# Two gMLP scalars: from GpSimd broadcasts to single elements that TensorE spreads over the partitions

## The chip, the cores and the metric

The kernel runs on one core of a Trainium2 chip. The metric is device time in microseconds (us). The chip's executions of this kernel fall into two close groups: in 35 runs of the kernel before, 7 lie at 667.7 to 668.0 us and 28 at 668.8 to 669.2. All count as fast.

The traces show where the groups part. The last 16 matmuls of the program took 1.25 us at a granted TensorE clock of 1.00 and 2.29 to 2.30 us at 0.50. From the last landing to the end that makes 3.60 to 3.76 us or 4.60 to 4.80 us.

## The reference

One decode step: layer norm, cached attention (batch 4, 32 heads, 4096 keys of 128) and a gMLP, summed.

```python
xn = _layernorm(x, axis=-1)
return x + _A_ref(xn, A_k_cache, A_v_cache, A_wq, A_wo) + _B_ref(xn, B_w_in, B_w_sp, B_b_sp, B_w_out)

def _B_ref(x, w_in, w_sp, b_sp, w_out):      # cut
    z = _gelu(jnp.einsum('bsd,df->bsf', x, w_in))
    z1 = z[..., :Fh]; z2 = _layernorm(z[..., Fh:], axis=-1)
    g = jnp.einsum('ts,bsf->btf', w_sp, z2) + b_sp[None, :, None]
    return jnp.einsum('bsf,fd->bsd', z1 * g, w_out)
```

The sequence has length 1, so `w_sp` and `b_sp` are one number each. They are the two scalars.

## The kernel before

The loads of weights, keys and values all go through SyncE's queue into one large buffer `kv`, in a fixed order. The scalars come through GpSimd, copied from one element in memory to all 128 partitions; much later a cast and one DVE instruction use them.

```python
nc.sync.dma_start(out=wq, in_=A_wq.rearrange("(p c) n -> p c n", c=DC))      # 5 MB, first load
nc.scalar.dma_start(out=x_bf, in_=x_flat)
...
sb_bf = const.tile([P, 2], BF16)
nc.gpsimd.dma_start(out=sb_bf[:, 0:1], in_=B_w_sp.rearrange("a b -> (a b)").to_broadcast((P, 1)))
nc.gpsimd.dma_start(out=sb_bf[:, 1:2], in_=B_b_sp.to_broadcast((P, 1)))
...                                                                         # w_in, w_out, then K and V
nc.gpsimd.tensor_copy(out=sb_f[:], in_=sb_bf[:])
...
nc.vector.tensor_scalar(out=t1[:], in0=t1[:], scalar1=sb_f[:, 0:1], scalar2=sb_f[:, 1:2],
                        op0=ALU.mult, op1=ALU.add)
nc.vector.tensor_tensor(out=uT[:, :, 0:B], in0=z1, in1=t1[:], op=ALU.mult)  # then the projection, L327
```

Of the kernel before, what the change touches and what calls it, by code (L numbers as in the profile page):

```python
# [11 lines left out]
F32 = mybir.dt.float32  # L12
BF16 = mybir.dt.bfloat16
# [3 lines left out]
def kernel(  # L17
# [19 lines left out]
    nc = tc.nc  # L37
    P = 128
# [26 lines left out]
    const = ctx.enter_context(tc.tile_pool(name="const", bufs=1))  # L65
# [11 lines left out]
    def misc_ps(shape, dtype):  # L77
        misc_ctr[0] += 1
        return ps_m.tile(shape, dtype, tag="misc", name=f"misc{misc_ctr[0]}")
# [20 lines left out]

    x_res = const.tile([32, NO2], BF16)
    nc.vector.memset(x_res[:], 0.0)
    sb_bf = const.tile([P, 2], BF16)
    nc.gpsimd.dma_start(out=sb_bf[:, 0:1], in_=B_w_sp.rearrange("a b -> (a b)").to_broadcast((P, 1)))
    nc.gpsimd.dma_start(out=sb_bf[:, 1:2], in_=B_b_sp.to_broadcast((P, 1)))
    sb_f = const.tile([P, 2], F32)

    n_in = DC * F2
    w_in = at_slot(2, n_in).rearrange("p (c f) -> p c f", c=DC)
# [3 lines left out]
    nf = (FC - 1) * P  # L113
    nc.sync.dma_start(out=w_out[:, 0:FC - 1, :], in_=B_w_out[0:nf, :].rearrange("(p c) n -> p c n", p=P))
    nc.sync.dma_start(out=w_out[:FL, FC - 1, :], in_=B_w_out[nf:Fh, :])


    seq = [("k", u) for u in range(B)]
# [121 lines left out]
    for hp in range(HP):  # L240
        nc.vector.tensor_copy(out=Pm[:, :, hp, :].rearrange("p (a w) j -> p a w j", w=2),
                              in_=ident_bf[:].rearrange("p (a j w) -> p a w j", a=2, w=2))
# [13 lines left out]
    for h in range(H):  # L256
        for c in range(DC):
            nc.tensor.matmul(q_ps[:, h, :], lhsT=wq[:, c, h * Dh:(h + 1) * Dh], rhs=xnT[:, c, :],  # L258
                             start=(c == 0), stop=(c == DC - 1))
# [3 lines left out]
    for kw in range(4):  # L263
        nc.tensor.matmul(q3_ps[:, kw, :], lhsT=Pm[:, kw, :, :].rearrange("p a j -> p (a j)"), rhs=q_bf[:],
                         start=True, stop=True)
# [5 lines left out]
    for part in range(2):  # L271
        for fc in range(FC):
            n = P if fc < FC - 1 else FL
            f0 = part * Fh
            for c in range(DC):
                if fc < FC - 1:
                    w = w_in[:, c, f0:f0 + nf].rearrange("p (f a) -> p a f", a=FC - 1)[:, fc, :]
                else:
                    w = w_in[:, c, f0 + nf:f0 + Fh]
                nc.tensor.matmul(zT_ps[:n, part, fc, :], lhsT=w,  # L280
                                 rhs=xnT[:, c, :], start=(c == 0), stop=(c == DC - 1))
# [3 lines left out]
    nc.vector.memset(uT[:], 0.0)  # L285
    nc.scalar.activation(out=zT[:, :, 0:FC - 1, :], in_=zT_ps[:, :, 0:FC - 1, :], func=ACT.Gelu_apprx_tanh)
    nc.scalar.activation(out=zT[:FL, :, FC - 1, :], in_=zT_ps[:FL, :, FC - 1, :], func=ACT.Gelu_apprx_tanh)
    nc.gpsimd.tensor_copy(out=sb_f[:], in_=sb_bf[:])
    z1 = zT[:, 0, :, :]
    z2 = zT[:, 1, :, :]  # L290
    st_in = const.tile([P, 2, FC, B], F32)
# [4 lines left out]
                     rhs=st_in[:].rearrange("p s c b -> p (s c b)"), start=True, stop=True)  # L296
# [26 lines left out]
    for fc in range(FC):  # L323
        n = P if fc < FC - 1 else FL
        nb = B if fc else 32
        for hf in range(NH):
            nc.tensor.matmul(proj[32 * hf:32 * hf + nb, 0:NO2], lhsT=uT[:n, fc, 0:nb],  # L327
                             rhs=w_out[:n, fc, hf * NO2:(hf + 1) * NO2], start=(fc == 0), stop=False)
# [151 lines left out]
    for i, item in enumerate(seq):  # L480
# [11 lines left out]
        g, b = divmod(u, B)  # L492
# [14 lines left out]
        else:  # L507
            emit_V(u)
            if u == NU - 2:
                for hf in range(NH):  # L510
                    nc.tensor.matmul(proj[32 * hf:32 * hf + B, 0:NO2], lhsT=ident_bf[:32, 4 * hf:32:8], rhs=x_res[:],
                                     start=False, stop=False)
# [39 lines left out]
```

## Time and profile before

| | before |
|---|---|
| time, median of 6 runs on the chip of the first comparison | 668.88 us |
| span of the profiled execution | 665.9 us |
| bytes on q1 / its share of the 16 transfer engines | 282.25 MB / 98.5% |
| DVE, the busiest compute engine | 54% of the span |
| last share of the last load landed | 662.15 us |

In the profile, PE is TensorE, DVE VectorE, ACT ScalarE, POOL GpSimd and SP SyncE. q1 is the queue of SyncE's loads and q0 that of GpSimd's.

The kernel is bound by its transfers, so an engine's share of busy time says little here. What to look for is time in which the transfer engines themselves stand still. The prediction shows the lines of the page, of the table of stretches and of the timeline for this.

Numbers that I use throughout come from the packet records of the trace (one row per packet: queue, start, length, bytes). *Idle per engine* is the time of a stretch less the packets' lengths in it, divided among 16 engines. The *mean end of the first K half* is the mean over the 16 engines of the end of each one's last line of that load, the first K load behind all the weights. It sums up everything that the engines have lost by then. The records name no engine: which packets follow each other on one engine is inferred from their ends and starts.

### The profile page before, as it was taken

What the parts mean: (1) busy time and instruction counts of PE and PEld (TensorE: products, weight loads), DVE (VectorE), ACT (ScalarE), POOL (GpSimd) and SP (SyncE); (2) the same over time, 40 slices, a digit from 0 to 9 for tenths busy, and PEclk for the clock granted to TensorE, in tenths of its full rate; (3) what the DMA queues carried; (4) which work ended last, traced back from release to release, by engine and by line L of the source; (5) the groups of instructions that cost most, each with busy time, mean ns of one, the idle gap of its engine ahead of it and who ended that gap; (6) DMA issues with size and microseconds to landing.
All of it is one profiled execution on the core that took longest, in us unless ns stands there. A gap on an engine that the chain in (4) does not pass through costs nothing.

```text
span 665.9 us, 6036 instructions
## 1 busy us (share of the span) xinstructions
PE 306.5 (46%) x2585; PEld 126.8 (19%) x2585; DVE 358.0 (54%) x318; ACT 93.3 (14%) x233; POOL 8.0 (1%) x27
## 2 busy tenths in 40 slices
PE   0656656526063546535425065551605336543355
PEld 0512211302011122211102022230201112122122
DVE  5179998446190749428356186743709165852002
ACT  1200000730200000450200000082020000046200
POOL 1000000000000000000000000000000000000000
PEclk9996787569578596676959587765867868677776
DMA  8999999999999999999999999999999999999996
GB/s 327 434 422 433 436 425 448 437 427 437 426 437 438 437 403 449 429 438 441 426 429 438 425 420 428 449 426 438 433 442 441 426 433 408 439 434 434 434 408 243
DMA packets 7874, 282.64 MB, mean 424 GB/s; under 512 B 948, under 2 KB 1320, under 8 KB 2088
## 3 DMA queue, kind: packets, MB, share of 16 engines
q1 hardware_dynamic: 7768, 282.25, 98.5%
q8 instruction: 20, 0.33, 0.2%
q14 instruction: 6, 0.05, 0.0%
q10 hardware_dynamic: 16, 0.01, 0.0%
q0 software_dynamic: 64, 0.00, 0.0%
HBM read 282.25 MB, written 0.01 MB: 424 GB/s over the span
## 4 chain that ended last, share of the span: by engine, by line
DMA 76%; DVE 10%; issue 10%; PE 2%; ACT 1%; DVEq 0%; SPq 0%; ACTq 0%
DMA kv<-in_A_k_cache_dram 66%; DVE kT L348 9%; DMA kv<-in_A_v_cache_dram 4%; DMA kv<-in_A_wo_dram 3%; DMA kv<-in_A_wq_dram 3%; PE misc L258 1%; ACT Zb L392 1%; ACT p L406 1%; DVE xd L414 1%; PE O L437 0%; PE proj L475 0%; PE x L410 0%; DVE om L457 0%; DVE m L366 0%; PE S L359 0%
## 5 line engine op out<-in xcount | busy, mean ns | idle before, releaser
L348 DVE STREAM_TRANSPOSE kT<-kv 128x2048 f32<-128x2048 f32 x128 | 283.4, 2277 | 134.2 <-DMA kv<-in_A_k_cache_dram 134.2
L359 PE MATMUL S<-kT,QZ 128*32 128x512 bf16 x1024 | 189.9, 505 | 237.5 <-DVE kT L348 237.5
L359 PEld LDWEIGHTS <-QZ 128*32 128x32 bf16 x1024 | 60.8, 112 | 359.9 <-issue 340.3
L437 PE MATMUL O<-kv,Zb 128*32 128x512 bf16 x1024 | 70.8, 431 | 34.4 <-DMA kv<-in_A_v_cache_dram 23.9
L392 ACT ACTIVATE Zb<-xd,MkE 32x256 bf16<-32x256 bf16 (+1 forms) x160 | 65.3, 454 | 108.3 <-PE O L437 99.1
L406 ACT ACTIVATE p<-S,negmax 128x512 bf16<-128x512 f32 x32 | 21.6, 694 | 398.2 <-DVE negmax L380 398.2
L444 DVE TENSOR_SCALAR R<-O,Mk 128x128 f32<-128x128 f32 x16 | 5.6, 351 | 106.2 <-PE O L437 106.2
L437 PEld LDWEIGHTS <-Zb 128*32 128x32 bf16 x1024 | 34.1, 106 | 69.2 <-issue 44.2
L414 DVE COPY xd<-x 32x512 bf16<-32x512 bf16 x32 | 22.0, 687 | 20.7 <-PE x L410 20.0
L410 PE MATMUL x<-IdP,p 128*128 128x128 bf16 x128 | 16.5, 309 | 25.2 <-ACT p L406 12.9
L410 PEld LDWEIGHTS <-p 128*128 128x128 bf16 x128 | 12.3, 140 | 30.2 <-ACT p L406 16.9
L454 PE MATMUL misc<-R,SelR 128*32 128x128 f32 x32 | 6.7, 293 | 24.0 <-DVE R L446 24.0
L446 DVE SCALAR_TENSOR_TENSOR R<-O,Mk,R 128x128 f32<-128x128 f32 x48 | 16.8, 351 | 1.7
L335 POOL COPY QZ<-q 32x32 bf16<-32x32 bf16 x16 | 5.1, 319 | 412.1 <-PE S L359 400.9
L475 PE MATMUL proj<-kv,oT 128*4 128x320 bf16 x64 | 8.4, 426 | 1.2 <-DMA kv<-in_A_wo_dram 1.0
L454 PEld LDWEIGHTS misc<-R,SelR 128*32 128x32 f32 x32 | 2.4, 112 | 31.4 <-DVE R L446 31.1
L366 DVE TENSOR_REDUCE m<-S 128x2 f32<-128x1024 f32 x4 | 4.9, 1225 | 6.0 <-PE S L359 6.0
L258 PE MATMUL misc<-xnT,kv 128*128 128x4 bf16 x160 | 4.4, 166 | 7.8 <-DMA kv<-in_A_wq_dram 7.8
L406 ACT ACTIVATION_READ_ACCUMULATOR p<-S,negmax 128x1 f32 x32 | 6.8, 212 | 0.0
L371 PE MATMUL misc<-dg,ones_f 128*128 128x256 f32 x8 | 3.0, 466 | 7.5 <-DVE dg L368 7.5
L457 DVE SCALAR_TENSOR_TENSOR om<-misc,rinv,MkH 32x1024 bf16<-32x1024 f32 x4 | 5.1, 1272 | 2.6 <-PE misc L454 2.6
L261 DVE CAST q_bf<-misc 128x128 bf16<-128x128 f32 x1 | 0.3, 292 | 11.3 <-PE misc L258 11.3
(92 smaller groups left out, 62.2 us busy)
## 6 DMA issues: line engine op xcount, KB each, us to landing
kv<-in_A_k_cache_dram SPq DMA_DIRECT2D x14, 4096.0 KB, 33.0
kv<-in_A_wq_dram SPq DMA_DIRECT2D x1, 5120.0 KB
kv<-in_A_v_cache_dram SPq DMA_DIRECT2D x1, 4096.0 KB, 38.4
kv<-in_A_wo_dram SPq DMA_DIRECT2D x2, 1280.0 KB, 28.7
kv<-in_B_w_in_dram SPq DMA_DIRECT2D x1, 2160.0 KB, 22.0
kv<-in_A_v_cache_dram SPq DMA_DIRECT2D x1, 2048.0 KB, 32.0
kv<-in_A_wo_dram SPq DMA_DIRECT2D x3, 640.0 KB, 20.7
kv<-in_A_v_cache_dram SPq DMA_DIRECT2D x1, 1536.0 KB
```

Of the source, the lines that this page charges most:

```text
L258: nc.tensor.matmul(q_ps[:, h, :], lhsT=wq[:, c, h * Dh:(h + 1) * Dh], rhs=xnT[:, c, :], start=(c == 0), stop=(c == DC - 1))
L348: nc.vector.transpose(kT[:].rearrange("p (t r) -> p t r", r=32), kw)
L359: nc.tensor.matmul(S_ps[32 * q:32 * q + 32, e], lhsT=QZ[:, b, 2 * kh + w, e, w0:w0 + 32], rhs=kb[:, i, :, e, :, w], start=(b == 0 and k < ...
L392: nc.scalar.activation(out=dst, in_=src, func=ACT.Copy, scale=MkE[r0:r0 + 32, e:e + 1])
L406: nc.scalar.activation(out=p_q[:, :, :, e, :], in_=S_ps[:, e, 8 * q:8 * q + 8, None, :].to_broadcast((P, 8, HP, M)), func=ACT.Exp, bias=ne ...
L410: nc.tensor.transpose(x[:, 8 * (q % 2) + t, :], p_q[:, t].rearrange("p r e m -> p (r e m)"), IdP[:])
L414: nc.vector.tensor_copy(out=xd[r0:r0 + 32, :, 16 * half:16 * half + 16], in_=x[r0:r0 + 32, :, r0:r0 + 32].rearrange("p t r -> p r t"))
L437: nc.tensor.matmul(O_ps[32 * q:32 * q + 32, :, :], lhsT=Zb[b % 2][:, w].rearrange("p h c -> p (h c)"), rhs=vv[:, w * 4 * Dh:(w + 1) * 4 * ...
L444: nc.vector.tensor_scalar(out=R, in0=O_ps[:, 0, :], scalar1=Mk4[:, 0:1], scalar2=None, op0=ALU.mult)
L446: nc.vector.scalar_tensor_tensor(out=R, in0=O_ps[:, c, :], scalar=Mk4[:, c:c + 1], in1=R, op0=ALU.mult, op1=ALU.add)
L454: nc.tensor.matmul(oh[:], lhsT=SelR[:, b].rearrange("p h b -> p (h b)"), rhs=state["R"][:, b, :], start=(b == 0), stop=(b == B - 1))
L475: nc.tensor.matmul(proj[32 * hf:32 * hf + B, 0:NO2], lhsT=oT[:, c, :], rhs=wo_t[g][:, c, hf * NO2:(hf + 1) * NO2], start=False, stop=(g == ...
```

## The change

The intent is to take the two broadcasts away from GpSimd: each scalar comes as a single element at the end of the first weights, on SyncE's queue, and one matmul with a row of ones copies both to 128 partitions.

```diff
-    sb_bf = const.tile([P, 2], BF16)
-    nc.gpsimd.dma_start(out=sb_bf[:, 0:1], in_=B_w_sp.rearrange("a b -> (a b)").to_broadcast((P, 1)))
-    nc.gpsimd.dma_start(out=sb_bf[:, 1:2], in_=B_b_sp.to_broadcast((P, 1)))
-    sb_f = const.tile([P, 2], F32)
 ...  (after the loads of w_in and w_out)
+    sb_bf = const.tile([1, 2], BF16)
+    nc.sync.dma_start(out=sb_bf[:, 0:1], in_=B_w_sp)
+    nc.sync.dma_start(out=sb_bf[:, 1:2], in_=B_b_sp[None, :])
 ...  (after the gelu)
-    nc.gpsimd.tensor_copy(out=sb_f[:], in_=sb_bf[:])
+    one_bf = const.tile([1, P], BF16)
+    nc.vector.memset(one_bf[:], 1.0)
+    sb_ps = misc_ps([P, 2], F32)
+    nc.tensor.matmul(sb_ps[:], lhsT=one_bf[:], rhs=sb_bf[:], start=True, stop=True)
+    sb_f = const.tile([P, 2], F32)
+    nc.vector.tensor_copy(out=sb_f[:], in_=sb_ps[:])
```

## The prediction

> **What bounds the kernel now.** I read the page first, its queues and its chain of waits.
>
> ```profile
> DMA packets 7874, 282.64 MB, mean 424 GB/s; under 512 B 948, under 2 KB 1320, under 8 KB 2088
> q1 hardware_dynamic: 7768, 282.25, 98.5%
> q0 software_dynamic: 64, 0.00, 0.0%
> DMA 76%; DVE 10%; issue 10%; PE 2%; ACT 1%; DVEq 0%; SPq 0%; ACTq 0%
> ```
>
> All 282.25 MB come through one hardware queue (q1), which keeps the 16 transfer engines busy for 98.5% of the span; DVE, the busiest compute engine, has 54%. q0 holds the two scalar broadcasts that the change removes, 64 tiny packets. A line of 40,960 bytes takes 1.514 us in the packet records, so 16 engines move 432.9 MB per ms and the bytes alone need 652.1 us of the span of 665.9. I also set the landing times on the semaphores against the issue times. After the first DMAs, whenever SyncE issues a load, earlier loads are still queued for at least 9.8 us more (the least, at 607.0 us). Between 15 and 655 us, no 5 us stretch has the transfer engines busy for less than 97%. So an issue or a compute step that shifts by a few us does nothing; only lost time of the transfer engines themselves counts, or a longer tail after the last landing at 662.2 us.
>
> Then the table of stretches, for where transfer time is lost (columns: stretch, its length, busy us and count for PE, PEld, DVE, ACT, POOL, the clock, the DMA share, GB/s):
>
> ```profile
> 4.00:5.00 1.00, 0.00 (x0) 0.00 (x0) 1.00 (x2) 0.00 (x0) 0.00 (x0) 1.00 1.15 492
> 5.00:6.00 1.00, 0.00 (x0) 0.00 (x0) 0.98 (x5) 0.00 (x0) 0.00 (x0) 1.00 0.11 41
> 6.00:8.00 2.00, 0.00 (x0) 0.00 (x0) 1.94 (x5) 0.29 (x1) 0.00 (x0) 1.00 0.74 307
> 12.00:15.00 3.00, 0.00 (x0) 0.00 (x0) 0.00 (x0) 0.00 (x0) 0.19 (x1) 1.00 1.01 437
> ```
>
> A packet's bytes are booked where it starts, so single us are rough. Still, there is a hole between 5 and 8 us in the first load (wq, 5 MB), and it is the only one before the end. In the packet records each engine runs its first two wq lines without a gap (mean end of the second 5.74 us), then stands idle, and starts the third at 7.42 us in the mean: 1.67 us of hole per engine. On all 16 engines the packet just ahead of that third line is one of q0, 16 bytes and 15 ns long, the first of the w_sp broadcast (6.53 us on the first engine, 8.52 on the last). No later pair of wq lines has such a gap.
>
> **What the Trainium skill says.** (1) DMA: Bandwidth & Descriptors, section "Queues, rings and completion order": each transfer engine round-robins between the queue rows it has work for, by packets. The trace agrees: the q0 packets stand one at a time between wq lines. (2) The same page, section "SWDGE vs HWDGE vs iDMA": for a DMA issued from GpSimd, software on its cores computes the descriptors and appends them to rings in SBUF that the engines drain; those issued from SyncE or ScalarE have them from hardware. Its first-byte figure for the software path, about 1 us, is not what this trace has: the issue starts at 1.23 us, the first packet at 6.53. So the page allows, but does not state, that an engine whose turn has come to q0 waits for q0's descriptors with wq ready behind it. (3) The same page, section "Why a DMA increments its semaphore by 16 and not by 1": on the hardware path a [1, 1] scalar goes to one engine, the lowest-numbered. No DMA of that shape is in this trace. (4) PSUM — Partial Sum Buffer, section "PSUM bank collisions raise a hardware error": banks must be guarded by semaphores. So the shared PSUM tile puts the new matmul in sequence with its neighbours; the trace has that form in the waits around the tile named misc.
>
> **Part 1: the two GpSimd broadcasts go.** GpSimd saves 0.68 + 0.54 us of issue and, at 13.6 us, a cast of 0.19 us. It is busy for 8.0 us in all, and its next needed result (QZ at 24.3 us) waits for DVE, so none of this counts. On the transfer side 64 packets go: they took 0.77 us summed over 16 engines, 0.05 us each. What counts is the hole. If q0 makes it, each engine starts its third line when the second is done, 1.67 us earlier in the mean. The end is set by the slowest engine: the first load's shares land at 16.22 to 18.04 us, and the last one is the engine that left the hole at 8.53. In the chaining of packets its gap was 1.5 us if it is the engine that also started late (second line done at 7.01), up to 3.0 if not. I choose 1.6 us. With the queue never empty afterwards, a gain at 8 us is still there at 662. Two waits on the broadcasts' semaphores in SyncE's closing list may also go, each sharing an instruction of about 0.06 us with another wait: at most 0.1 us.
>
> **Part 2: two single-element DMAs on SyncE.** Neighbouring issues take 0.40 to 0.79 us each, so the first K half is issued at about 4.4 us instead of 3.19 (2 x 0.6). Earlier loads keep the queue busy until 26.5 us: nothing. Their own transfer is two small packets on one engine, at 9 to 15 ns as for small packets here: nothing. They sit behind w_out and so land at 24 to 26.5 us. The hardware queues' DMAs use eight semaphores in turn, and an issue waits for the semaphore's earlier user. With two more DMAs ahead, the second half of K unit 1 takes the one of w_in (lands 23.17) instead of that of x (2.5), so its issue moves from 22.97 to about 23.2 us, with 32.6 us of loads queued. Nothing again; later loads keep the eighth DMA before them as before.
>
> **Part 3: TensorE spreads the scalars.** The timeline of the gMLP:
>
> ```profile
> 13.62 0.19 POOL L288 CAST sb_f<-sb_bf 128x2 f32<-128x2 bf16 x1 [9.74 <-DMA sb_bf<-in_B_b_sp_dram]
> ...
> 28.12 0.16 ACT L287 ACTIVATE zT<-misc 96x8 f32<-96x8 f32 x1
> ...
> 28.32 0.18 DVE L292 COPY st_in<-zT 128x28 f32<-128x28 f32 x1 [4.09 <-ACT zT L287]
> 28.41 0.18 DVE L293 TENSOR_TENSOR st_in<-zT 128x28 f32<-128x28 f32 x1
> ...
> 28.73 0.64 PE L295 MATMUL misc<-st_in,ones_f 128*128 128x56 f32 x2 [0.76 <-DVE st_in L293]
> ...
> 31.11 0.30 DVE L314 TENSOR_SCALAR t<-t,sb_f 128x28 f32<-128x28 f32 x1
> 31.45 0.19 DVE L316 TENSOR_TENSOR uT<-zT,t 128x28 bf16<-128x28 f32 x1
> 31.69 2.05 PE L327 MATMUL proj<-kv,uT 128*32 128x320 bf16 x14 [2.31 <-DVE uT L316]
> ...
> 36.21 4.50 DVE L348 STREAM_TRANSPOSE kT<-kv 128x2048 f32<-128x2048 f32 x2 [4.58 <-DMA kv<-in_A_k_cache_dram]
> 38.58 1.89 PE L359 MATMUL S<-kT,QZ 128*32 128x512 bf16 x8 [4.84 <-DVE kT L348]
> ```
>
> The new matmul's PSUM tile is a third user between zT_ps and st_ps in a pool of one buffer: it must wait for the gelu's read (28.28 us), and the statistics matmul must wait for the copy out. Cost: one small bf16 matmul at 0.17 us (as L258 and L280), one small copy out of PSUM at 0.17 (as xnT, L193), and two or three hand-overs of about 0.08 (as between L293 and L295): 0.17 + 0.17 + 0.24 = about 0.6 us on the chain to uT. The memset of 128 elements is 0.1 us in DVE's early slack. The chain ends in the projection, at 33.74 us; the next work of PE starts at 38.58 after 4.84 us idle, that of DVE at 36.21 after 4.58 us. If the first K half comes 1.6 us earlier, DVE still has about 3 us to spare for 0.6. The K load that waits for L327 is issued at 33.78 with 31.4 us of loads queued. Cost for the end: nothing.
>
> **Sum:** 668.84 - 1.6 - 0.05 = 667.2 us if the hole belongs to q0, about 668.8 if not.
>
> **The rivals.** (a) The hole is not q0's: it may be how the first load's hardware descriptors arrive, as it comes after exactly two lines on each engine. Against it: the q0 packet ahead of the third line on all 16 engines, and no gap later. For it: the q0 packet itself lasts 15 ns, so the link is order, not duration. Time: 668.8. (b) The scheduler puts the new matmul early in PE's order, ahead of the q projection (18.1) or of the z projection (24.3), and PE stands until the scalars land at about 26. Then the gMLP chain would be 2 to 8 us later and DVE's first K transposes up to about 4 us late. The queue holds 30 us of loads at this stage, and DVE needs 8.89 us per K half against some 9.7 between landings, so it catches up: 668.8, or 667.2 with the hole gone. (c) The scalars fail to land before 28.3 us behind the other queued loads, so that the gMLP waits for them: the same slack takes some 3 to 4 us, and more is not likely as w_out is complete at 26.5. (d) SyncE's later issues starve the engines: against it are the 9.8 us of least backlog.
>
> **Range and chances.** I give the hole to q0 at about two in three, and its worth at the end 1.0 to 2.2 us, as engines gain unequally. Weighted towards that, I say 667.4 us. The range runs from 666.2 (a gain of 2.2, with 0.4 of run-to-run spread; the three runs before span 0.8) to 669.2 (no gain, a bad run). Two per cent is 13 us, eight times the hole: within 2% 0.98, faster 0.01, slower 0.01.
>
> **What would show it.** Right: no q0 row; the stretch from 5 to 8 us above 400 GB/s; wq landed at about 16.5 us instead of 18.04, and the first K half's transposes starting near 34.7 instead of 36.21; the statistics matmul about 0.6 us later after the gelu; the same shift of about 1.6 us at the end. Wrong: the hole is there without q0 (rival a), or it is gone but the last landing is still near 662 us, so that some engine gave it back. A new PE wait on the scalars between 18 and 28 us is rival (b) or (c). A time above 670 us would mean that a backlog ran out, which I do not expect.

## The result, and the profile after

The changed kernel takes 666.88 us (median of 6 runs, 666.07 to 667.36) against 668.88 us (668.02 to 669.06). The ratio is 0.9971, with a 95% interval of 0.9958 to 0.9984. Ratios are the mean time of one kernel's fast runs over that of the other's of the same rounds, so not quite the ratio of the medians. By the interval it is a real gain of about 2 us.

The page of the changed kernel, its packets, its main queue and its chain of waits:

```profile
DMA packets 7814, 282.63 MB, mean 425 GB/s; under 512 B 888, under 2 KB 1260, under 8 KB 2028
q1 hardware_dynamic: 7772, 282.25, 98.7%
DMA 76%; DVE 10%; issue 10%; PE 2%; ACT 1%; DVEq 0%; SPq 0%; ACTq 0%
```

The row of q0 is gone. q1 has four packets more, two elements and two semaphore counts. The chain by engine is as before to the per cent: nothing has moved between limits.

The stretches of the first load in the changed kernel (columns as in the prediction, the last two are the DMA share and GB/s):

```profile
4.00:5.00 1.00, 0.00 (x0) 0.00 (x0) 1.00 (x2) 0.00 (x0) 0.00 (x0) 1.00 1.16 492
5.00:6.00 1.00, 0.00 (x0) 0.00 (x0) 1.00 (x6) 0.00 (x0) 0.00 (x0) 1.00 1.33 573
6.00:8.00 2.00, 0.00 (x0) 0.00 (x0) 1.94 (x6) 0.29 (x1) 0.00 (x0) 1.00 0.85 369
12.00:15.00 3.00, 0.00 (x0) 0.00 (x0) 0.00 (x0) 0.00 (x0) 0.00 (x0) 1.00 0.78 334
```

From 5 to 6 us the engines now start 573 GB/s of lines where they started 41. The stretches above and below 433 GB/s only show that a line is booked where it starts, and that all engines now start theirs at the same times. In the packet records the idle time per engine between 5 and 10 us falls from 1.65 us to none, and no stretch of 5 us from 10 to 640 us differs by more than about 0.01 us. The mean end of the first K half goes from 34.44 to 32.74 us, a gain of 1.70. The last share of the last load lands at 660.60 instead of 662.15 us, a gain of 1.55, and the span ends 1.6 us earlier. Both profiled executions have the short tail, so they compare like with like: 667.67 us before and 666.07 after. The six timed runs of each kernel have one in the faster group, 668.02 and 666.07. That the timing shows 2.0 and the traces 1.6 thus lies in the execution profiled before, which is not one of the six; why it was 0.35 us faster is not known.

The timeline of the gMLP in the changed kernel (start, length, engine, line, operation; in brackets the idle time and what ended it):

```profile
26.16 0.16 ACT L286 ACTIVATE zT<-misc 96x8 f32<-96x8 f32 x1
...
26.37 0.16 PE L291 MATMUL misc<-sb_bf,one_bf 1*128 1x2 bf16 x1 [0.36 <-ACT zT L286]
26.44 0.18 DVE L298 TENSOR_TENSOR st_in<-zT 128x28 f32<-128x28 f32 x1
26.57 0.16 DVE L293 COPY sb_f<-misc 128x2 f32<-128x2 f32 x1
...
26.78 0.67 PE L300 MATMUL misc<-st_in,ones_f 128*128 128x56 f32 x2 [0.25 <-DVE sb_f L293]
...
29.68 2.05 PE L332 MATMUL proj<-kv,uT 128*32 128x320 bf16 x14 [2.23 <-DVE uT L321]
...
34.40 6.70 DVE L353 STREAM_TRANSPOSE kT<-kv 128x2048 f32<-128x2048 f32 x3 [4.77 <-DMA kv<-in_A_k_cache_dram]
```

The new matmul waits for the gelu as foreseen. But DVE prepares the statistics (L298) while PE spreads the scalars, and the copy of the scalars (L293) comes just behind. The statistics matmul starts 0.46 us after the gelu's end (26.32), against 0.45 us before (28.28 to 28.73). The detour costs the chain nothing. The first K transposes start at 34.40 instead of 36.21 us.

### The profile page after: what moved, and what is told of

The parts are those of the page before. It is cut to its first block, busy times and chain, and to the rows that moved or that the text cites. A ratio compares the mean times of both kernels' runs of the same rounds, so it can differ in the third digit from the quotient of the medians.

```text
span 664.3 us, 6032 instructions
## 1 busy us (share of the span) xinstructions
PE 315.6 (48%) x2586; PEld 128.4 (19%) x2586; DVE 358.1 (54%) x320; ACT 93.3 (14%) x233; POOL 6.2 (1%) x24
## 4 chain that ended last, share of the span: by engine, by line
DMA 76%; DVE 10%; issue 10%; PE 2%; ACT 1%; DVEq 0%; SPq 0%; ACTq 0%
DMA kv<-in_A_k_cache_dram 66%; DVE kT L353 9%; DMA kv<-in_A_v_cache_dram 4%; DMA kv<-in_A_wo_dram 3%; DMA kv<-in_A_wq_dram 2%; PE misc L257 1%; ACT Zb L397 1%; ACT p L411 1%; DVE xd L419 1%; PE O L442 0%; PE proj L480 0%; PE x L415 0%; PE S L364 0%; DVE om L462 0%; DVE m L371 0%
## 5 line engine op out<-in xcount | busy, mean ns | idle before, releaser
L364 PE MATMUL S<-kT,QZ 128*32 128x512 bf16 x1024 | 196.5, 519 | 233.0 <-DVE kT L353 233.0
L364 PEld LDWEIGHTS <-QZ 128*32 128x32 bf16 x1024 | 62.2, 114 | 359.9 <-issue 342.5
L442 PE MATMUL O<-kv,Zb 128*32 128x512 bf16 x1024 | 73.4, 443 | 30.5 <-DMA kv<-in_A_v_cache_dram 21.0
L415 PE MATMUL x<-IdP,p 128*128 128x128 bf16 x128 | 16.5, 309 | 25.2 <-ACT p L411 12.9
```

Of the source, the lines that this page charges most:

```text
L364: nc.tensor.matmul(S_ps[32 * q:32 * q + 32, e], lhsT=QZ[:, b, 2 * kh + w, e, w0:w0 + 32], rhs=kb[:, i, :, e, :, w], start=(b == 0 and k < ...
L415: nc.tensor.transpose(x[:, 8 * (q % 2) + t, :], p_q[:, t].rearrange("p r e m -> p (r e m)"), IdP[:])
L442: nc.tensor.matmul(O_ps[32 * q:32 * q + 32, :, :], lhsT=Zb[b % 2][:, w].rearrange("p h c -> p (h c)"), rhs=vv[:, w * 4 * Dh:(w + 1) * 4 * ...
```

## The experiments

So the hole in the first load is the whole gain. The open question is what in the two GpSimd broadcasts makes it. My theory was the software queue q0: each engine would wait once for its descriptors. The rivals were the tiny transfers themselves and, later, the single source address. Each experiment is the changed kernel plus one dead thing (work whose result nobody uses), or the kernel before with one edit; e4_long_chain alone adds steps to the live chain. The three sets of runs were on three chips, with medians of the kernel before of 668.92, 668.87 and 669.00 us.

### Both ways at once (e1_both)

```diff
 (changed kernel)
+    sb_old = const.tile([P, 2], BF16)
+    nc.gpsimd.dma_start(out=sb_old[:, 0:1], in_=B_w_sp.rearrange("a b -> (a b)").to_broadcast((P, 1)))
+    nc.gpsimd.dma_start(out=sb_old[:, 1:2], in_=B_b_sp.to_broadcast((P, 1)))
 ...
+    sb_old_f = const.tile([P, 2], F32)
+    nc.gpsimd.tensor_copy(out=sb_old_f[:], in_=sb_old[:])
```

> The changed kernel with the two GpSimd broadcasts put back beside the new path, into a tile that only GpSimd's old cast reads. Theory (the software queue q0 makes the hole of 1.67 us in the first load): the hole comes back, wq lands near 18 us, the first K transposes start near 36.2 us and the time is that of the kernel before, ratio 0.999 to 1.001. Rival (the gain of 2.0 us comes from the new way of spreading the scalars, or from what GpSimd no longer computes): wq lands near 16.1 us and the ratio stays near 0.997.

667.92 us, ratio 0.9994 (0.9982 to 1.0006). The hole is back in the table of stretches:

```profile
5.00:6.00 1.00, 0.00 (x0) 0.00 (x0) 1.00 (x6) 0.00 (x0) 0.00 (x0) 1.00 0.26 82
6.00:8.00 2.00, 0.00 (x0) 0.00 (x0) 1.95 (x6) 0.29 (x1) 0.00 (x0) 1.00 0.70 287
```

Idle per engine is 1.47 us, the mean end of the first K half 34.61 us, the first K transposes start at 36.28. The gain belongs to the removal of the broadcasts, and the new path neither gives nor takes anything.

### The same broadcasts on SyncE's queue (e2_sync_bcast)

```diff
 (kernel before; the two lines move behind the loads of w_out)
-    nc.gpsimd.dma_start(out=sb_bf[:, 0:1], ...to_broadcast((P, 1)))
-    nc.gpsimd.dma_start(out=sb_bf[:, 1:2], ...to_broadcast((P, 1)))
+    nc.sync.dma_start(out=sb_bf[:, 0:1], ...to_broadcast((P, 1)))
+    nc.sync.dma_start(out=sb_bf[:, 1:2], ...to_broadcast((P, 1)))
```

> The kernel before with one edit: the two broadcasts to 128 partitions are issued from SyncE behind the first weights instead of from GpSimd; GpSimd's cast stays, TensorE spreads nothing. Theory (only the software queue costs): no q0, no hole, wq lands near 16.1 us, ratio near 0.997 as with the whole change. Rival (256 two-byte writes cost something wherever they are queued, so that single elements matter): a smaller gain, ratio 0.998 to 1.000, with a gap of 0.5 us or more behind w_out in the queue.

668.31 us, ratio 0.9986 (0.9974 to 0.9999). My theory missed here. There is no q0 and no hole at 5 us, but a new one where the broadcasts stand in the queue:

```profile
22.00:24.00 2.00, 1.61 (x33) 1.61 (x33) 0.34 (x1) 0.00 (x0) 1.34 (x4) 1.00 0.51 168
```

The engines are idle for 1.16 us each between 19 and 25 us, and the first K half ends at 33.99 us in the mean, 1.25 later than in the changed kernel. So a broadcast costs on a hardware queue too.

### GpSimd broadcasts later (e3_late_q0)

```diff
 (changed kernel, ahead of the q projection)
+    sb_old = const.tile([P, 2], BF16)
+    nc.gpsimd.tensor_copy(out=sb_old[:], in_=wq[:, 0, 0:2])        # waits until wq has landed
+    nc.gpsimd.dma_start(out=sb_old[:, 0:1], in_=B_w_sp...to_broadcast((P, 1)))
+    nc.gpsimd.dma_start(out=sb_old[:, 1:2], in_=B_b_sp.to_broadcast((P, 1)))
```

> The changed kernel with two dead GpSimd broadcasts added that are issued only after wq has landed (about 16 us), when the hardware queue holds more than 15 us of loads. Theory A (the first use of q0 stalls each engine once, whenever it comes): no hole at 5 to 8 us, but one of 1 to 2 us per engine some 4 to 5 us after the issue, and a time as before, ratio 0.999 to 1.001. Theory B (the stall needs the engines at their start, with few descriptors prefetched): no hole anywhere, ratio near 0.997.

668.66 us, ratio 0.9999 (0.9987 to 1.0011). The hole has moved with them: issued at 16.5 us, they leave 1.26 us of idle time per engine between 19 and 25 us, and the mean end of the first K half is 34.36 us. It is nothing of the engines' start.

### A longer gMLP chain (e4_long_chain)

```diff
 (changed kernel, ahead of the use of the scalars)
+    for _ in range(16):
+        nc.vector.tensor_scalar(out=t1[:], in0=t1[:], scalar1=1.0, scalar2=None, op0=ALU.mult)
```

> The changed kernel with 16 dependent DVE multiplications by 1.0 put into the gMLP chain ahead of the use of the scalars, about 0.2 us each, 3.2 us in all. Theory (4.8 us of idle DVE and 5.0 us of idle PE ahead of the first K transposes hide the chain): the projection starts 3.2 us later, near 33 us, the first K transposes still at 34.4 us, time as the changed kernel, ratio near 0.997. Rival (the chain sets the pace of the K stage): 2 to 3 us slower than the changed kernel, ratio near 1.001.

667.05 us, ratio 0.9976 (0.9964 to 0.9988), as the changed kernel. The timeline of this run:

```profile
33.22 2.05 PE L334 MATMUL proj<-kv,uT 128*32 128x320 bf16 x14 [5.65 <-DVE uT L323]
34.38 4.50 DVE L355 STREAM_TRANSPOSE kT<-kv 128x2048 f32<-128x2048 f32 x2 [1.22 <-DMA kv<-in_A_k_cache_dram]
```

The projection starts 3.5 us later, DVE's wait ahead of the transposes shrinks from 4.77 to 1.22 us, and the transposes start as early as ever. The slack that the prediction relied on is there.

### One element through GpSimd (e5_one_q0)

```diff
 (changed kernel)
+    sb_old = const.tile([1, 2], BF16)
+    nc.gpsimd.dma_start(out=sb_old[:, 0:1], in_=B_w_sp)
```

> The changed kernel with one single GpSimd DMA added, of one element into one partition, that nobody reads. Theory (each engine stalls once, when its turn first comes to q0; a GpSimd DMA puts at least its semaphore count on all 16 engines): the hole at 5 to 8 us is as large as with the two broadcasts, 1.3 to 1.7 us per engine, the first K transposes start near 36.2 us, ratio 0.999 to 1.000. Rival (the hole is the time of the 64 or more small packets, or falls only on the engine that has data): 0.1 us or less in the mean, ratio near 0.997, or between the two if one engine alone is late by 1.5 us.

667.04 us, ratio 0.9969 (0.9957 to 0.9982). q0 is in use, and in the packet records one of its packets stands between the second and the third wq line of all 16 engines (from 5.52 us), exactly where the hole was. But there is no hole:

```profile
q0 software_dynamic: 32, 0.00, 0.0%
...
5.00:6.00 1.00, 0.00 (x0) 0.00 (x0) 1.00 (x5) 0.00 (x0) 0.00 (x0) 1.00 1.53 655
```

The mean end of the first K half is 32.89 us. My theory of the software queue fell here.

### Eight broadcasts through GpSimd (e6_eight_q0)

```diff
 (changed kernel)
+    sb_old = const.tile([P, 8], BF16)
+    for i in range(8):
+        nc.gpsimd.dma_start(out=sb_old[:, i:i + 1], in_=B_w_sp...to_broadcast((P, 1)))
```

> The changed kernel with eight dead GpSimd broadcasts to 128 partitions instead of none. Theory (one stall at the first use, what follows is prefetched): one hole of 1.3 to 1.7 us per engine, no more than 0.5 us of further idle time up to 30 us. Rival (every GpSimd DMA stalls the engines anew): four times the hole of the kernel before or more, 6 us per engine, and a time near 673 us.

One run, state unknown: 672.65 us. The first K half ends at 38.25 us in the mean, 5.5 us later than in the changed kernel, or 0.7 us for each broadcast. That is not one stall at the first use, which the theory wanted. It is near the rival's 6 us and 673 us: further broadcasts stall anew. That every GpSimd DMA does so, as the rival had it, is already out by e5_one_q0.

### The broadcasts on ScalarE's queue (e7_scalar_bcast)

```diff
 (kernel before, same place)
-    nc.gpsimd.dma_start(out=sb_bf[:, 0:1], ...)
-    nc.gpsimd.dma_start(out=sb_bf[:, 1:2], ...)
+    nc.scalar.dma_start(out=sb_bf[:, 0:1], ...)
+    nc.scalar.dma_start(out=sb_bf[:, 1:2], ...)
```

> The kernel before with the two broadcasts issued from ScalarE instead of from GpSimd, at the same place. Theory (the stall belongs to the software queue; 256 two-byte writes cost about 1.2 us per engine wherever hardware queues them, as the broadcasts on SyncE did): idle time of 0.9 to 1.4 us per engine among the first lines of wq, first K transposes at 35.7 to 36.3 us, ratio 0.998 to 0.9995. Rival 1 (any second queue makes the engines wait): 2.5 us or more, slower than before. Rival 2 (two-byte writes interleave with the 40 KB lines for free): no idle time, ratio near 0.997.

668.25 us, ratio 0.9995 (0.9982 to 1.0009), with the first K half ending at 33.95 us: 1.2 us lost. The expectation missed in form: only 0.4 us of it is idle time between packets, and the mean wq line takes 1.71 us instead of 1.62 in the changed kernel, which over 8 lines is another 0.7 us. The loss can hide inside the packets.

### One broadcast on SyncE's queue (e8_half_bcast)

```diff
 (changed kernel, behind the two single elements)
+    sb_old = const.tile([P, 2], BF16)
+    nc.sync.dma_start(out=sb_old[:, 0:1], in_=B_w_sp...to_broadcast((P, 1)))
```

> The changed kernel with one dead broadcast of a scalar to 128 partitions on SyncE's queue behind the two single elements. Theory (the cost on the hardware queue goes with the number of two-byte packets, 1.24 us per engine for 16 of them): 0.5 to 0.7 us of idle time per engine between 19 and 25 us for 8 of them. Rival (a fixed cost of switching to small packets): 1.2 us again.

One run, state unknown: 668.42 us. Half the packets of e2_sync_bcast cost as much: the first K half ends at 34.04 us in the mean (1.30 lost). A cost per two-byte packet does not fit this. Neither two-byte packets nor the queue was a good account by now. What the runs that lost time had in common was that all 16 engines read one address; tiny transfers of any kind were not out yet, and the next runs part the two.

### The same GpSimd packets from 128 addresses (e9_q0_apart)

```diff
 (changed kernel, at the old place)
+    sb_old = const.tile([P, 2], BF16)
+    nc.gpsimd.dma_start(out=sb_old[:, 0:1], in_=B_w_out[0:P, 0:1])
+    nc.gpsimd.dma_start(out=sb_old[:, 1:2], in_=B_w_out[P:2 * P, 0:1])
```

> The changed kernel with two dead GpSimd DMAs at the old place, each of 128 two-byte elements into 128 partitions, but read from 128 addresses 1,280 bytes apart instead of from one. After the last four runs the software queue as such no longer explains the hole (a single element through it cost nothing). Theory S (many reads of one address by all engines at once are what stalls): no hole, first K half landing as in the changed kernel (mean end of its lines 32.7 us), ratio near 0.997. Theory T (tiny two-byte transfers stall, wherever they read): a hole of 1.2 to 1.7 us per engine, mean end near 34.4 us, ratio near 0.9995.

667.05 us, ratio 0.9973 (0.9959 to 0.9986). This is the cleanest comparison. q0 carries the same 64 packets as in the kernel before, of the same sizes (32 of 16 bytes, 32 semaphore counts), at the same place:

```profile
q0 software_dynamic: 64, 0.00, 0.0%
...
5.00:6.00 1.00, 0.00 (x0) 0.00 (x0) 1.00 (x6) 0.00 (x0) 0.00 (x0) 1.00 1.53 656
```

Only the addresses that they read differ (and with them the tensor, but e10_q0_wide and e12_sync_wide below read the same tensor and do lose time), and there is no hole; the mean end of the first K half is 32.86 us.

### GpSimd broadcasts of 512 bytes (e10_q0_wide)

```diff
 (changed kernel, at the old place)
+    sb_old = const.tile([P, 2, 256], BF16)
+    nc.gpsimd.dma_start(out=sb_old[:, 0, :], in_=B_w_out[0:1, 0:256].to_broadcast((P, 256)))
+    nc.gpsimd.dma_start(out=sb_old[:, 1, :], in_=B_w_out[1:2, 0:256].to_broadcast((P, 256)))
```

> The changed kernel with two dead GpSimd broadcasts at the old place, each of one row of 512 bytes to 128 partitions: still one source for all engines, but no tiny writes. Their bytes alone are 0.3 us of transfer. Theory S (one source address): a hole of 1.2 us or more beyond the bytes, mean end of the first K half's lines 34.2 us or later, ratio near 0.9995 or above. Theory T (tiny transfers): 0.3 to 0.5 us in all, mean end near 33.1 us, ratio near 0.9975.

669.14 us, ratio 1.0001 (0.9989 to 1.0014). The mean end of the first K half is 34.88 us, 2.14 lost, of which the bytes are 0.3. There is no idle time between the packets. Instead each of the 32 packets of 4,096 bytes takes 0.913 us in the records, where the rate of a wq line (40,960 bytes in 1.514 us) would give 0.151. A loss of much the same size is booked as long packets:

```profile
q0 software_dynamic: 64, 0.13, 0.3%
...
5.00:6.00 1.00, 0.00 (x0) 0.00 (x0) 1.00 (x6) 0.00 (x0) 0.00 (x0) 1.00 1.66 217
```

### The same pair on SyncE's queue (e11_sync_apart, e12_sync_wide)

```diff
 (changed kernel, behind the two single elements; one of)
+    nc.sync.dma_start(out=sb_old[:], in_=B_w_out[0:P, 0:1])                              # e11
+    nc.sync.dma_start(out=sb_old[:], in_=B_w_out[0:1, 0:256].to_broadcast((P, 256)))     # e12
```

> The changed kernel with one dead SyncE DMA of 128 two-byte elements from 128 addresses 1,280 bytes apart, at the place where the dead broadcast of one element cost 1.3 us. Theory S (one source address): mean end of the first K half's lines near 32.8 us. Theory T (tiny transfers): near 34.0 us.

> The changed kernel with one dead SyncE broadcast of one 512-byte row to 128 partitions at the same place. Its bytes are 0.15 us. Theory S (one source address): mean end of the first K half's lines near 34.0 us or later. Theory T (tiny transfers): near 32.9 us.

e11_sync_apart takes 666.96 us (ratio 0.9968, 0.9955 to 0.9980), e12_sync_wide 668.17 us (0.9986, 0.9974 to 0.9999). The mean ends are 32.80 and 34.15 us. Apart again costs nothing and a common source costs 1.4 us. The stretch that holds these packets, first in e11_sync_apart:

```profile
22.00:24.00 2.00, 1.60 (x33) 1.60 (x33) 0.35 (x1) 0.00 (x0) 1.31 (x4) 1.00 1.40 515
```

and in e12_sync_wide:

```profile
22.00:24.00 2.00, 1.76 (x35) 1.76 (x35) 0.19 (x1) 0.00 (x0) 1.34 (x4) 1.00 0.69 203
```

All runs side by side (loss: mean end of the first K half less that of the changed kernel, 32.74 us):

| extra transfers | queue | source | loss, us | ratio to before |
|---|---|---|---|---|
| none (changed kernel) | | | 0 | 0.9971 |
| none, long chain | | | 0.06 | 0.9976 |
| 1 element | GpSimd | one reader | 0.15 | 0.9969 |
| 2 x 128 elements | GpSimd | 128 addresses | 0.12 | 0.9973 |
| 128 elements | SyncE | 128 addresses | 0.06 | 0.9968 |
| 2 broadcasts (e1_both) | GpSimd | one address each | 1.87 | 0.9994 |
| 2 broadcasts, late | GpSimd | one address each | 1.62 | 0.9999 |
| 2 broadcasts of 512 B | GpSimd | one row each | 2.14 | 1.0001 |
| 8 broadcasts | GpSimd | one address | 5.51 | one run |
| 2 broadcasts (without the change) | SyncE | one address each | 1.25 | 0.9986 |
| 1 broadcast | SyncE | one address | 1.30 | one run |
| 1 broadcast of 512 B | SyncE | one row | 1.41 | 0.9986 |
| 2 broadcasts (without the change) | ScalarE | one address each | 1.21 | 0.9995 |

The losses fall into two clear groups, and they last to the end: the last load lands at 660.40 to 660.60 us in the five runs that lost 0.15 us or less, at 661.67 to 662.99 in the seven that lost 1.2 to 2.1, and at 666.12 with eight broadcasts. The ratios follow, but less sharply, as timed runs of the two groups enter them in different shares (two of five runs of e5_one_q0 are in the faster group, none of e4_long_chain): the nearest two, 0.9976 and 0.9986, have overlapping intervals, and within a group they tell nothing apart. No run points to a version faster than the changed kernel.

## Why the prediction was right or wrong

**What bounds the kernel: right.** The queue is never empty, so the 1.70 us gained in the first load is still 1.55 us at the last landing, and 3.5 us put into the compute chain did nothing. One reading was off without effect: the least backlog at an issue is 9.3 us, at 133.9 us (the load ahead lands at 143.2), not 9.8 at 607.0.

**Part 1, the size: right.** The hole was measured at 1.67 us per engine and I took 1.6 us for the end; the trace gives 1.55 to 1.6 and the timed medians 2.0. The time is 666.88 us against 667.4 foreseen, inside the range. The point was set high for the case that the hole would stay. That the size held though its cause did not is luck: the sum counts the hole whoever makes it, and the change took away the queue and the shared reads together. Moved to SyncE's queue (e2_sync_bcast), the broadcasts left q0 as well, and the same working would have foreseen the whole gain; the first K half came only 0.45 us earlier than before.

**Part 1, the cause: wrong.** The step that failed is "an engine whose turn has come to q0 waits for q0's descriptors with wq ready behind it". One element through q0 on all 16 engines costs no hole, and the same packets as before, read from 128 addresses, cost none either. What costs is a source that all engines read at once. On GpSimd's and SyncE's queues this is shown against the same number of elements from separate addresses (losses of 1.87 against 0.12 us, and 1.30 against 0.06); on ScalarE's queue the broadcasts cost as much (1.21 us), but that control was not run. I had drawn the cause from order: the q0 packet ahead of the third line on all engines. Rival (a) said as much, that a packet of 15 ns shows order and not duration; its own cause, the arrival of the first load's descriptors, is out too, as the hole went with the broadcasts and came back with them, late ones included. The record of a packet did not show the wait for what it read.

**Part 2, no cost: right.** The issues took 0.34 and 0.22 us instead of the 0.4 to 0.79 I took from their neighbours, so the first K half was issued at 3.71 us (4.4 foreseen). The elements landed at 23.4 and 23.6 us, some 2.8 us ahead of the matmul. The second half of K unit 1 did wait for w_in (21.18 us) and was issued at 21.25, without effect.

**Part 3, the term was mis-sized:** 0.6 us more foreseen from the gelu to the statistics matmul, 0.01 us measured. I had set matmul, copy and hand-overs in a row with the statistics; the scheduler ran them beside DVE's two instructions. Rivals (b) and (c) did not occur: PE waits for the gelu, not for the scalars.

**The marks for right: all seen.** No q0; wq landed at 16.08 us (16.5 foreseen); transposes from 34.40 us (34.7); the hole gone. One mark was badly put: "above 400 GB/s from 5 to 8 us" comes to (573 + 2 x 369) / 3 = 437, but with lines booked at their starts single stretches swing from 334 to 573.

**What stays open.** Why reads of one address stall the engines, in memory or on the way to it, no run shows. Nor is it clear why two broadcasts of different scalars on SyncE cost no more than one (1.25 and 1.30 us), while eight of one scalar on GpSimd cost 5.5. Nor is it known how near the addresses must lie: only one shared element or row, and elements 1,280 bytes apart, were run. Broadcasts from on-chip memory were not tried.

## What to carry to other kernels

When a kernel is bound by its transfers, a broadcast of a few bytes from memory to all partitions can cost more than a microsecond of every transfer engine, far more than its bytes (here 1.30 us for 256 bytes): load the value once and spread it on the chip, in an engine's slack. Before blaming a queue for a hole, change one thing at a time: send the same packets through the same queue from other addresses, and other packets through it. And measure such losses by when the engines finish a later load, since the wait may be booked as a gap, as a long packet, or as longer neighbours.

## What the Trainium skill lacked or had wrong

- DMA: Bandwidth & Descriptors: its section "Rules for kernel authors" says that a source may repeat (a broadcast), with no word of a cost. Here a broadcast of one element or of one 512-byte row to 128 partitions cost each engine 1.3 to 1.4 us on SyncE's queue, two cost 1.6 to 2.1 us on GpSimd's, and the same count of elements from addresses 1,280 bytes apart at most 0.12 us.
- The same page, its table of specifications: about 1 us to the first byte for GpSimd's path. In the run with one element the issue started at 1.21 us and the first q0 packet came at 5.52 us. It stood behind the second wq line of its engine, though most first lines had ended at about 4 us, 2.8 us after the issue. Whether q0 had nothing ready by then, or the engines already held their second lines, no run shows, so the figure is not refuted; behind a full queue the first packet took 4.3 us.
- Perfetto Trace Analysis, section "DMA Optimizations", gives DMAs below 2 KB a significant overhead per transfer. On a queue that is never empty none was seen: the two single elements left no idle time, and with 128 two-byte elements the first K half ended 0.06 us later, no more than in the long-chain run, which adds no transfer.
